# A new opening for a fused attention and feed-forward kernel: first k on two queues, another order of loads and steps

## The chip, the cores and the metric

The kernel runs on one core of a Trainium2 chip. The metric is the device time in microseconds (us), lower is better. A profiled execution has a span (first to last instruction of the program), which is shorter than its time: by 2.1 us in the kernel before (332.03 against 329.9 us). All runs here are of the fast state: the granted clock of TensorE was 0.995 to 1.0 of full speed.

## The reference, cut to what matters

```python
def _attn_ref(q, k, v):              # q, k, v: 8 batches x 8 heads x 576 x 64, float32
    scores = np.matmul(q, k.transpose(0, 1, 3, 2)) / np.sqrt(64)
    rel = pos[:, None] - pos[None, :]
    scores = np.where((rel >= 0) & (rel < 64), scores, -1000000000.0)   # window of 64
    ...                              # softmax, then @ v
def _moe_ref(x, w_gate, w_val, w_out):   # x: 4608 tokens x 512; d_ff = 1536
    g = x @ w_gate
    return (g / (1.0 + np.exp(-g)) * (x @ w_val)) @ w_out
```

Attention with a window of 64 gives x; a gated feed-forward follows. The kernel computes in bfloat16.

## The kernel before

Tokens are worked in 36 pieces of 128 ("chunks" of attention, counted from 0) and 9 pieces of 512 (the feed-forward's: piece 0 is chunks 0 to 3, piece 1 is chunks 4 to 7). A table of steps writes the program in order; each engine runs its own part of it in that order, and waits are worked out from who reads and writes what. LOADS are the first DMA issues, STEPS the opening of the program; after it a regular loop runs to the end.

```python
LOADS = """
f:0 init q:0 kq:1 kq:2 v:1 v:0 kq:3 v:2 v:3 w:7:9 w:1:2 w:5:6 kq:4 kq:5 w:3:4 ...
"""                      # kq:n = q and k of chunk n; w:a:b = columns a*128..b*128 of w_gate, then of w_val
STEPS = """
warm:45:64 B:0 B:1 ca:0:0 cd:0:1 T:0:1 T:0:0 ea:0:1 TQ:0 ld:8 wo:0:6 ed:0:0 qa:0 W:1 TQ:1 S:0 ...
"""
# W: a fill that computes nothing; T, TQ, TK: transposes (TensorE) of the first k, of q, of k
# qa/qd, ka/kd, xa/xd: evictions by ACT / DVE;  B: mask as a matmul;  S: scores and exp;  M: mask on DVE
# A0, A1: attention times v;  N: normalize (DVE);  X: transpose of x
# F:c:f:t0:t1: gate and value matmuls of block f for columns t0..t1 of piece c;  U: its two DVE steps
# TD, XD: transposes by DMA;  O: output matmuls
...
def first_load(self, n):         # k of chunk 0, float32, in two halves
    for u in range(2):
        ...
        self.g.op("sp", lambda e, d=d, a=a: e.dma_start(d, a), writes=[("ff", n, u)], dma=True)
...
def load_w(self, which, a, b):   # float32 in HBM to bfloat16 in SBUF, issued by POOL, like q, k and v
    self.g.op("pool", lambda e: e.dma_start(d, s), writes=[("W" + which, f) for f in range(a, b)], dma=True)
```

The softmax here doesn't subtract the row's maximum and nothing guards it: scores larger than these inputs give would overflow.

Of the kernel before, what the change touches and what calls it, by code (L numbers as in the profile page):

```python
# [7 lines left out]
B, H, S, D = 8, 8, 576, 64  # L8
DM, DFF = H * D, 1536
T = B * S  # L10
# [139 lines left out]
class _Kernel:  # L150
# [9 lines left out]
    LAST = NFC  # L160
    NI = 1
    LOADS = """
    f:0 init q:0 kq:1 kq:2 v:1 v:0 kq:3 v:2 v:3 w:7:9 w:1:2 w:5:6 kq:4 kq:5 w:3:4 w:4:5 w:6:7 v:5 w:2:3 v:6
    v:4 w:9:10 w:0:1 kq:6 v:7 kq:7 w:10:12
    """
    STEPS = """
    warm:45:64 B:0 B:1 ca:0:0 cd:0:1 T:0:1 T:0:0 ea:0:1 TQ:0 ld:8 wo:0:6 ed:0:0 qa:0 W:1 TQ:1 S:0 qd:1 TK:1
    ld:9 kd:1 W:1 TQ:2 S:1 qd:2 TK:2 kd:2 W:2 S:2 W:1 A0:0 A0:1 A1:0 A1:1 ld:10 N:0 TQ:3 B:3 qa:3 N:1 TK:3 X:0
    ka:3 xa:0 M:2 W:1 S:3 X:1 A0:2 xd:1 A1:2 ld:11 N:2 W:1 A0:3 A1:3 N:3 W:1 X:2 F:0:7:0:256 xd:2 U X:3
    F:0:8:0:384 xd:3 F:0:1 U U F:0:5 U TK:4 TQ:4 ld:12 ka:4 TQ:5 F:0:7:256:512 qd:4 TK:5 qa:5 F:0:8:384:512 U  # L170
    S:4 U F:0:3 kd:5 M:4 S:5 U F:0:4 M:5 U F:0:6 U F:0:2 U A0:4 A0:5 A1:4 ld:13 wo:6:12 A1:5 F:0:9 N:4 N:5 X:4
    F:0:0 U xa:4 X:5 U TK:6 xa:5 TQ:6 ld:14 F:1:0:0:128 ka:6 U F:1:1:0:256 qa:6 TQ:7 U F:1:2:0:256 qd:7 S:6
    TK:7 U F:1:3:0:256 kd:7 F:0:10 M:6 U U A0:6 S:7 A1:6 ld:15 TQ:8 TK:8 N:6 F:0:11 M:7 ka:8 qd:8 X:6 A0:7
    xa:6 S:8 U A1:7 ld:16 F:1:4:0:384 N:7 F:1:5:0:384 U X:7 U TQ:9 xa:7 F:1:6:0:384 M:8 qa:9 TK:9 U F:1:7 kd:9
    TD:10 U A0:8 S:9 A1:8 ld:17 F:1:8 N:8 M:9 X:8 TQ:11 xa:8 F:1:9 U qd:11 A0:9 TK:11 U A1:9 ka:11 F:1:10 N:9
    TK:12 U X:9 ka:12 TQ:12 F:1:11 xd:9 qd:12 TD:13 S:10 U S:12 F:1:0:128:512 M:10 F:1:1:256:512 M:12 A0:10 U
    S:11 A1:10 U F:1:2:256:512 F:1:3:256:512 N:10 F:1:4:384:512 U XD:10 F:1:5:384:512 O:0:0 U U U M:11 O:0:1
    A0:11 S:13 A1:11 O:0:2 N:11 M:13 X:11 O:0:3 xd:11 F:1:6:384:512 U TD:14 TD:15
    """

    def __init__(self, nc, q, k, v, wg, wv, wo, out):
# [103 lines left out]
    def first_load(self, n):  # L285
        (_, b, s, L), = self.segs(128 * n, 128)
        for u in range(2):
            d = self.ff[n][64 * u:64 * u + 64].rearrange("p h j d -> p h (j d)")
            a = self.k[b, 4 * u:4 * u + 4, s:s + L, :].rearrange("h (p j) d -> p h (j d)", j=2)
            self.g.op("sp", lambda e, d=d, a=a: e.dma_start(d, a), writes=[("ff", n, u)], dma=True)  # L290

    def cast(self, n, half, eng):
        hs = slice(2 * half, 2 * half + 2)
# [489 lines left out]
```

## Time and profile before

| | before |
|---|---|
| time, median of 4 runs | 332.23 us (331.72 to 332.55) |
| span of the profiled run | 329.9 us |
| TensorE busy | 320.5 us, 97% |
| first feed-forward matmul | 17.48 us |
| its second half (waits for Wv) | 18.09 us |
| second feed-forward ends | 20.06 us (20.28 in the profile, where a record is missing; see below) |
| first feed-forward of piece 2 (first thing after STEPS) | 83.31 us |

The lines of the profile are in the prediction.

### The profile page before, as it was taken

How to read it: one execution, taken by the hardware profiler on the slowest of the kernel's cores; microseconds unless marked ns; L12 is line 12 of the kernel's file. 1: busy time of each engine (PE TensorE's matmuls, PEld its weight loads, DVE VectorE, ACT ScalarE, POOL GpSimd, SP SyncE). 2: the span in 40 equal slices, each digit the busy share in tenths (PEclk: the TensorE clock that was granted, in tenths of full speed). 3: DMA queues.
4: the chain of work that ended last, by engine and by line, in shares of the span. 5: the costliest groups of instructions: out<-in, count | busy, mean ns of one | idle time of the engine just before them, and what ended most of it. 6: DMA issues, size and time to landing. Idle time of an engine off the chain costs nothing.

```text
span 329.9 us, 8342 instructions
## 1 busy us (share of the span) xinstructions
PE 320.5 (97%) x3505; PEld 166.2 (50%) x3543; DVE 217.0 (66%) x457; ACT 136.0 (41%) x247; POOL 116.5 (35%) x145
## 2 busy tenths in 40 slices
PE   7999999999999999999999999999999999999996
PEld 5565665564455444544445454545454544444444
DVE  5689999992467758585857676767676766555520
ACT  3736566453344344343425252525343432332222
POOL 8999999966017506060706060100000000000000
PEclk9999999999999999999999999999999999999999
DMA  9999999999999989999999999442424111100012
GB/s 104 163 169 171 160 184 156 160 156 181 189 173 142 167 155 105 152 90 167 90 169 82 175 75 184 67 111 42 120 35 128 34 64 34 64 34 32 32 63 99
DMA packets 169365, 38.56 MB, mean 117 GB/s; under 512 B 160368, under 2 KB 164848, under 8 KB 169328
## 3 DMA queue, kind: packets, MB, share of 16 engines
q0 software_dynamic: 123600, 18.75, 84.0%
q1 hardware_dynamic: 45584, 19.21, 29.2%
q8 instruction: 28, 0.46, 0.6%
q14 instruction: 9, 0.07, 0.1%
q10 hardware_dynamic: 144, 0.07, 0.1%
HBM read 37.75 MB, written 9.44 MB: 143 GB/s over the span
## 4 chain that ended last, share of the span: by engine, by line
PE 95%; DVE 2%; issue 1%
PE ps L602 56%; PE ps L635 27%; PE ps L421 3%; PE ps L534 2%; PE ps L309 2%; PE ps L471 2%; PE ps L665 1%; PE ps L568 1%; PE ps L401 1%; DVE xb L493 1%; PE ps L357 0%; DVE kT L301 0%; DVE mask L267 0%; DVE hT L613 0%; DVE pt L437 0%
## 5 line engine op out<-in xcount | busy, mean ns | idle before, releaser
L611 DVE SCALAR_TENSOR_TENSOR uu<-sig,ps 128x512 bf16<-128x512 bf16 (+3 forms) x117 | 75.4, 644 | 66.1 <-ACT sig L608 65.8
L602 PE MATMUL ps<-xT,Wv 128*128 128x512 bf16 (+3 forms) x466 | 112.4, 363 | 0.1
L602 PE MATMUL ps<-xT,Wg 128*128 128x512 bf16 (+3 forms) x447 | 108.1, 362 | 2.0 <-issue 0.6
L608 ACT ACTIVATE sig<-ps 128x512 bf16<-128x512 f32 (+3 forms) x117 | 66.0, 565 | 88.8 <-PE ps L602 88.7
L635 PE MATMUL ps<-Wo,hT 128*128 128x512 bf16 x405 | 94.6, 379 | 2.2 <-issue 2.1
L613 DVE SCALAR_TENSOR_TENSOR hT<-uu,ps 128x512 bf16<-128x512 bf16 (+3 forms) x117 | 75.6, 646 | 4.0
L371 POOL DMA_DIRECT2D va<-in_v_dram x40 | 39.7, 1026 | 89.4 <-PE ps L534 87.3
L602 PEld LDWEIGHTS ps<-xT,Wv 128*128 128x128 bf16 x468 | 44.9, 98 | 49.1 <-DVE hT L613 0.5
L602 PEld LDWEIGHTS ps<-xT,Wg 128*128 128x128 bf16 x468 | 43.9, 98 | 46.1 <-DMA xT<-xb 0.5
L635 PEld LDWEIGHTS ps<-Wo,hT 128*128 128x128 bf16 x420 | 39.9, 98 | 46.6
L431 ACT ACTIVATE pt<-ps 128x512 bf16<-128x512 f32 x72 | 37.8, 600 | 26.7 <-PE ps L421 26.6
L647 ACT ACTIVATE ost<-ps 128x512 f32<-128x512 f32 x35 | 20.9, 597 | 66.2 <-PE ps L635 66.0
L283 POOL DMA_DIRECT2D qn<-in_q_dram x40 | 40.7, 1037 | 2.6 <-issue 1.8
L283 POOL DMA_DIRECT2D kn<-in_k_dram x39 | 40.0, 1047 | 0.3 <-DMA kn<-in_k_dram 0.3
L437 DVE TENSOR_TENSOR pt<-pt,mask 128x512 bf16<-128x512 bf16 x66 | 24.3, 419 | 0.2
L556 DVE TENSOR_TENSOR xb<-ps,rp 128x448 bf16<-128x448 f32 (+1 forms) x36 | 18.5, 513 | 1.2
L553 DVE RECIPROCAL rp<-ps 128x7 f32<-128x7 f32 (+1 forms) x36 | 6.7, 187 | 15.5 <-PE ps L534 15.5
L421 PE MATMUL ps<-qT,kT 64*64 64x64 bf16 (+1 forms) x864 | 16.0, 205 | 0.4 <-ACT kT L299 0.2
L421 PEld LDWEIGHTS ps<-qT,kT 64*64 64x64 bf16 x864 | 12.4, 109 | 7.5 <-DVE hT L613 4.2
L534 PE MATMUL ps<-va,pt 64*64 64x65 bf16 x728 | 11.5, 193 | 0.1
L493 DVE TENSOR_TENSOR xb<-ps,rc 128x256 bf16<-128x256 f32 x24 | 10.2, 425 | 0.8
L534 PEld LDWEIGHTS ps<-va,pt 64*64 64x64 bf16 x728 | 9.4, 108 | 0.6 <-DVE hT L613 0.4
(50 smaller groups left out, 104.9 us busy)
## 6 DMA issues: line engine op xcount, KB each, us to landing
out_dram<-ost SPq DMA_DIRECT2D x35, 256.0 KB, 2.8
qn<-in_q_dram POOLq DMA_DIRECT2D x32, 128.0 KB, 6.7
va<-in_v_dram POOLq DMA_DIRECT2D x32, 128.0 KB, 6.4
kn<-in_k_dram POOLq DMA_DIRECT2D x31, 128.0 KB, 7.2
Wo<-in_moe_w_out_dram POOLq DMA_DIRECT2D x2, 768.0 KB, 12.1
Wg<-in_moe_w_gate_dram POOLq DMA_DIRECT2D x8, 128.0 KB, 5.5
Wv<-in_moe_w_val_dram POOLq DMA_DIRECT2D x8, 128.0 KB, 5.6
Wg<-in_moe_w_gate_dram POOLq DMA_DIRECT2D x2, 256.0 KB, 5.7
```

The costliest lines, as they stand in the source:

```text
L283: self.g.op("pool", lambda e, d=d, a=a: e.dma_start(d, a), writes=ks, dma=True)
L371: g.op("pool", lambda e, d=d, a=a: e.dma_start(d, a), writes=ks, dma=True)
L421: r = e.matmul(sv[h][o:o + 64, c, q0:q1], self.kT[ps, c, kk:kk + 64], qT[ps, c, q0:q1], start=not biased, stop=not biased or c == 3 and kk ...
L431: g.op("act", lambda e, po=po, si=si: e.activation(po, si, ACTF.Exp, scale=SCALE), reads=[bk], writes=[pk])
L437: "dve", lambda e: e.tensor_tensor(po, po, m, ALU.mult), reads=[pk, "mask"], writes=[pk]))
L534: r = e.matmul(bb[b][0][ws, 65 * sl:65 * sl + 65], self.pt[(n + j) % self.NP][ks, h, ws], vv[ks, h, 0:65], start=m == q[0], stop=m == q[-1])
L602: r = e.matmul(bank[:, 0:n], W[:, kk, f * 128:f * 128 + 128], xT[:, kk, t0:t1], start=(kk == 0), stop=(kk == NK - 1))
L608: g.op("act", lambda e: e.activation(sig[:, 0:n], G[:, 0:n], ACTF.Tanh, scale=0.5), reads=[gk], writes=[("sig", i)])
L611: g.op("dve", lambda e: e.scalar_tensor_tensor(uu[:, 0:n], sig[:, 0:n], 1.0, G[:, 0:n], ALU.add, ALU.mult), reads=[("sig", i), gk], writes ...
L613: g.op("dve", lambda e: e.scalar_tensor_tensor(hT[:, f, t0:t1], uu[:, 0:n], 0.5, V[:, 0:n], ALU.mult, ALU.mult), reads=[("uu", i), vk], wr ...
L635: r = e.matmul(OB[:, :], hT[:, f, 128 * u:128 * u + 128], self.Wo[:, f, :], start=(f == 0), stop=(f == NF - 1))
L647: g.op("act", lambda e: e.activation(ost[:, :], OB[:, :], ACTF.Copy), reads=[ok], writes=[("ost", io)])
```

## The change

Its intent: load the first k faster, start attention of the first chunks sooner, and re-search the order of loads and steps. The description also speaks of one DMA transpose fewer.

```diff
-    f:0 init q:0 kq:1 kq:2 v:1 v:0 kq:3 v:2 v:3 w:7:9 w:1:2 w:5:6 kq:4 kq:5 w:3:4 w:4:5 w:6:7 v:5 w:2:3 v:6
-    v:4 w:9:10 w:0:1 kq:6 v:7 kq:7 w:10:12
+    f:0 init q:0 kq:2 kq:1 v:1 v:0 kq:3 v:2 kq:6 v:3 w:7:9 kq:5 kq:4 w:2:3 w:4:5 w:0:2 v:4 kq:7 w:9:10 v:5
+    w:10:12 w:5:7 w:3:4 v:7 v:6
...
-    warm:45:64 B:0 B:1 ca:0:0 cd:0:1 T:0:1 T:0:0 ea:0:1 TQ:0 ld:8 wo:0:6 ed:0:0 qa:0 W:1 TQ:1 S:0 qd:1 TK:1
...                                             (the whole table of steps is replaced)
+    warm:45:96 B:0 ca:0:0 cd:0:1 T:0:0 T:0:1 ea:0:0 ed:0:1 TQ:0 ld:8 B:1 qa:0 TQ:2 S:0 qd:2 TK:2 kd:2 W:1 TQ:1
+    qa:1 W:1 TK:1 ld:9 wo:0:6 ka:1 W:2 S:1 B:2 A0:0 S:2 A1:0 N:0 A0:1 A1:1 ld:10 TQ:3 N:1 W:1 X:0 qa:3 TK:3
+    xa:0 kd:3 W:1 X:1 A0:2 xa:1 S:3 A1:2 ld:11 TQ:6 N:2 W:1 TK:6 ka:6 M:3 W:1 X:2 qa:6 xd:2 W:1 A0:3 A1:3
+    F:0:7:0:384 N:3 U X:3 TQ:5 xa:3 F:0:8:0:384 qd:5 TK:5 U TQ:4 ka:5 F:0:7:384:512 F:0:8:384:512 qd:4 S:6
...
-            self.g.op("sp", lambda e, d=d, a=a: e.dma_start(d, a), writes=[("ff", n, u)], dma=True)
+            self.g.op(("sp", "act")[u], lambda e, d=d, a=a: e.dma_start(d, a), writes=[("ff", n, u)], dma=True)
```

More of the change, by code (lines that the diff above doesn't have):

```diff
@@ L162 @@
     LOADS = """
-    f:0 init q:0 kq:1 kq:2 v:1 v:0 kq:3 v:2 v:3 w:7:9 w:1:2 w:5:6 kq:4 kq:5 w:3:4 w:4:5 w:6:7 v:5 w:2:3 v:6
-    v:4 w:9:10 w:0:1 kq:6 v:7 kq:7 w:10:12
+    f:0 init q:0 kq:2 kq:1 v:1 v:0 kq:3 v:2 kq:6 v:3 w:7:9 kq:5 kq:4 w:2:3 w:4:5 w:0:2 v:4 kq:7 w:9:10 v:5
+    w:10:12 w:5:7 w:3:4 v:7 v:6
     """
     STEPS = """
-    warm:45:64 B:0 B:1 ca:0:0 cd:0:1 T:0:1 T:0:0 ea:0:1 TQ:0 ld:8 wo:0:6 ed:0:0 qa:0 W:1 TQ:1 S:0 qd:1 TK:1
-    ld:9 kd:1 W:1 TQ:2 S:1 qd:2 TK:2 kd:2 W:2 S:2 W:1 A0:0 A0:1 A1:0 A1:1 ld:10 N:0 TQ:3 B:3 qa:3 N:1 TK:3 X:0
@@ L169 @@
-    ka:3 xa:0 M:2 W:1 S:3 X:1 A0:2 xd:1 A1:2 ld:11 N:2 W:1 A0:3 A1:3 N:3 W:1 X:2 F:0:7:0:256 xd:2 U X:3
-    F:0:8:0:384 xd:3 F:0:1 U U F:0:5 U TK:4 TQ:4 ld:12 ka:4 TQ:5 F:0:7:256:512 qd:4 TK:5 qa:5 F:0:8:384:512 U
-    S:4 U F:0:3 kd:5 M:4 S:5 U F:0:4 M:5 U F:0:6 U F:0:2 U A0:4 A0:5 A1:4 ld:13 wo:6:12 A1:5 F:0:9 N:4 N:5 X:4
-    F:0:0 U xa:4 X:5 U TK:6 xa:5 TQ:6 ld:14 F:1:0:0:128 ka:6 U F:1:1:0:256 qa:6 TQ:7 U F:1:2:0:256 qd:7 S:6
-    TK:7 U F:1:3:0:256 kd:7 F:0:10 M:6 U U A0:6 S:7 A1:6 ld:15 TQ:8 TK:8 N:6 F:0:11 M:7 ka:8 qd:8 X:6 A0:7
@@ L174 @@
-    xa:6 S:8 U A1:7 ld:16 F:1:4:0:384 N:7 F:1:5:0:384 U X:7 U TQ:9 xa:7 F:1:6:0:384 M:8 qa:9 TK:9 U F:1:7 kd:9
-    TD:10 U A0:8 S:9 A1:8 ld:17 F:1:8 N:8 M:9 X:8 TQ:11 xa:8 F:1:9 U qd:11 A0:9 TK:11 U A1:9 ka:11 F:1:10 N:9
-    TK:12 U X:9 ka:12 TQ:12 F:1:11 xd:9 qd:12 TD:13 S:10 U S:12 F:1:0:128:512 M:10 F:1:1:256:512 M:12 A0:10 U
-    S:11 A1:10 U F:1:2:256:512 F:1:3:256:512 N:10 F:1:4:384:512 U XD:10 F:1:5:384:512 O:0:0 U U U M:11 O:0:1
-    A0:11 S:13 A1:11 O:0:2 N:11 M:13 X:11 O:0:3 xd:11 F:1:6:384:512 U TD:14 TD:15
+    warm:45:96 B:0 ca:0:0 cd:0:1 T:0:0 T:0:1 ea:0:0 ed:0:1 TQ:0 ld:8 B:1 qa:0 TQ:2 S:0 qd:2 TK:2 kd:2 W:1 TQ:1
@@ new lines @@
+    qa:1 W:1 TK:1 ld:9 wo:0:6 ka:1 W:2 S:1 B:2 A0:0 S:2 A1:0 N:0 A0:1 A1:1 ld:10 TQ:3 N:1 W:1 X:0 qa:3 TK:3
+    xa:0 kd:3 W:1 X:1 A0:2 xa:1 S:3 A1:2 ld:11 TQ:6 N:2 W:1 TK:6 ka:6 M:3 W:1 X:2 qa:6 xd:2 W:1 A0:3 A1:3
+    F:0:7:0:384 N:3 U X:3 TQ:5 xa:3 F:0:8:0:384 qd:5 TK:5 U TQ:4 ka:5 F:0:7:384:512 F:0:8:384:512 qd:4 S:6
+    TK:4 ld:12 U U F:0:2 kd:4 M:6 S:4 U S:5 F:0:4 M:4 F:0:0 M:5 U A0:4 F:0:1 U U A1:4 ld:13 wo:6:12 TK:7 TQ:7
+    ka:7 F:0:9 N:4 qa:7 U X:4 A0:5 xa:4 S:7 A1:5 ld:14 F:0:10 N:5 M:7 U X:5 F:0:11 xd:5 U F:0:5 U F:0:3 U A0:6
@@ new lines @@
+    A0:7 A1:6 ld:15 A1:7 TQ:8 F:0:6 N:6 N:7 qa:8 X:6 TK:8 ld:16 xa:6 TQ:9 U X:7 ka:8 F:1:0:0:256 TK:9 xa:7
+    qd:9 S:8 U F:1:1 kd:9 M:8 F:1:2 U U A0:8 S:9 A1:8 ld:17 F:1:3 N:8 TD:10 U X:8 F:1:4 xd:8 U TQ:11 F:1:5 M:9
+    qa:11 U F:1:6 U A0:9 TK:11 A1:9 ka:11 F:1:7 N:9 U X:9 TK:12 xa:9 TQ:12 F:1:8 kd:12 qd:12 TD:13 S:10 U S:12
+    F:1:9 M:10 A0:10 M:12 S:11 A1:10 F:1:10 U N:10 F:1:11 U XD:10 F:1:0:256:512 U O:0:0 U M:11 A0:11 S:13
+    A1:11 O:0:1 N:11 M:13 X:11 O:0:2 xd:11 O:0:3 TD:14 TD:15
```

## The prediction

> **What bounds the kernel now.** I read the page first, then busy time by stretches, then the order of time of the first 34 us, then single transfers from issue to landing. The page says who is busy and who ends the run.
>
> ```profile
> PE 320.5 (97%) x3505; PEld 166.2 (50%) x3543; DVE 217.0 (66%) x457; ACT 136.0 (41%) x247; POOL 116.5 (35%) x145
> ...
> PE 95%; DVE 2%; issue 1%
> ```
>
> TensorE holds 97% of the span and 95% of the chain that ended last. The time is therefore a sum: the tensor work that has to be done plus the time in which TensorE does none of it. The change adds and removes hardly any tensor work, so I look for the lost time. The table by stretches has the span, then busy time and instruction count per engine:
>
> ```profile
> 0.00:20.28 20.28, 17.62 (x340) 11.69 (x341) 12.84 (x47) 9.78 (x18) 19.24 (x28) 1.00 1.71 141
> 20.28:82.86 62.58, 61.27 (x849) 36.73 (x859) 51.83 (x124) 33.41 (x66) 56.60 (x69) 1.00 2.00 167
> 82.86:329.90 247.04, 241.59 (x2318) 117.76 (x2343) 152.35 (x287) 92.79 (x163) 40.63 (x49) 1.00 0.87 102
> ```
>
> From 20.28 us to 82.86 us (the rest of the stage that the change rewrites) TensorE is idle 62.58 - 61.27 = 1.3 us, so little can be won there. Part of that 1.3 us is not even real: after many small matmuls a group of 4 shows only 3, and the missing record (216 ns) leaves a hole. After 82.86 us the step list ends and the program is the same. What is left is the first 20.28 us. The order of time shows what happens there:
>
> ```profile
> 6.87 0.63 PE L357 MATMUL ps<-wz 128*128 128x512 bf16 x1
> ...
> 8.80 0.38 PE L357 MATMUL ps<-wz 128*128 128x512 bf16 x1
> ...
> 17.48 0.60 PE L602 MATMUL ps<-xT,Wg 128*128 128x256 bf16 x4
> ...
> 18.09 0.33 PEld L602 LDWEIGHTS ps<-xT,Wv 128*128 128x128 bf16 x4 [0.29 <-DMA Wv<-in_moe_w_val_dram]
> ...
> 18.76 0.81 PE L602 MATMUL ps<-xT,Wg 128*128 128x384 bf16 x4
> ...
> 20.28 0.81 PE L602 MATMUL ps<-xT,Wg 128*128 128x512 bf16 x3
> ```
>
> L357 are fills that keep the clock up and compute nothing. The first feed-forward matmul starts at 17.48 us, its second half waits for the first Wv at 18.09 us, and from 18.54 us on TensorE is nearly full. What decides the opening is when the first pair of Wg and Wv pieces lands. They are issued by POOL, which is never idle from 1.24 us on:
>
> ```profile
> 7.47 0.93 POOL L283 DMA_DIRECT2D qn<-in_q_dram  x1
> 8.34 0.94 POOL L283 DMA_DIRECT2D kn<-in_k_dram  x1
> ...
> 10.93 0.84 POOL L377 DMA_DIRECT2D Wg<-in_moe_w_gate_dram  x1
> 11.67 0.83 POOL L377 DMA_DIRECT2D Wv<-in_moe_w_val_dram  x1
> 12.40 0.84 POOL L377 DMA_DIRECT2D Wg<-in_moe_w_gate_dram  x1
> ```
>
> From start to start a q, k or v load of one chunk takes 8.34 - 7.47 = 0.87 us of POOL, a weight load 11.67 - 10.93 = 0.74 us whatever its width. The view of Wv gives 6.4 us from issue to landing for the one issued at 11.67 us: 18.05 us, just where TensorE's wait of 0.29 us ends. The Wg ahead of it has 5.8 us: 16.7 us.
>
> **The Trainium skill.** "DMA: Bandwidth & Descriptors", section "Issuing engines are not separate DMA queues": DMAs from several engines share the same 16 DMA engines, and issuing from more than one saves only the sequencer's issue time. The trace lets me size that for the first k. Its two halves are issued on SP at 0.74 and 1.54 us; the view of ff has 2.7 us to landing for one and 4.1 us for the other, so they land at 3.4 and 5.6 us. The second was issued after POOL's first q (1.24 us) and shares the engines with it. "TensorE: Matmul & The Clock Gate", section "Part 1: The HAM clock gate": the full clock comes after about 3.4 us of sustained activity in a free-running window. The trace agrees in kind: the same fill takes 0.63 us at 6.87 us and 0.38 us at 8.80 us. "Trainium Kernel Development and Optimization", section "Performance Expectations": matmul busy time is a bad metric as matmuls are pipelined. Here too: a 512-column matmul lasts 0.38 us but starts every 0.216 us (24 of them take 5.18 us in the chain), so I count starts.
>
> **The change part by part.** (1) ff on two queues. The second half goes out on ACT about 0.8 us earlier and lands, by estimate, at 3.6 to 4.3 us in place of 5.6. The mask set-up on DVE lasts to 4.6 us and the longer warm-up (45 matmuls of 96 columns in place of 64; at the low clock 53 ns x 96/64 = 80 ns each, 3.6 us) to 4.62 us. So the first transposes start at some 5.1 to 5.5 us in place of 6.03: 0.5 to 0.9 us won. But q of chunk 0 lands at 6.2 us (4.9 us after its issue at 1.24), so scores of chunk 0 win about 0.3 us, and what comes next waits for loads on POOL: chunk 2's at the old times of chunk 1, and k of chunk 1 at the old time of k of chunk 2, 9.56 us. Nothing of the 0.5 us reaches the first feed-forward.
>
> (2) The order of loads. The old list has 11 loads of q, k, v ahead of the first weights, the new one 13 (q and k of chunk 6 were put ahead). That is 2 x 0.87 = 1.73 us: Wg lands at 16.7 + 1.73 = 18.4 us, Wv at 18.05 + 1.73 = 19.8 us. **This is the step I trust most.**
>
> (3) The first feed-forward. New list: 384 columns at once (1.30 us) in place of 256 (0.87 us). Its second half starts at 19.8 us and ends at 20.45 us (4 x 162 ns). Then transpose X of chunk 3 (4 x 56 ns = 0.22), q of chunk 5 (0.22), second feed-forward of 384 columns (1.30): 22.2 us. Now compare the useful work. The old kernel had at 20.28 us everything of chunks 0 to 3, plus 0.87 + 1.30 of feed-forward. The new one has at 22.2 us the same plus 0.43 (384 against 256 columns) plus the transposes of chunk 6 (0.44) plus q of chunk 5 (0.22) = 1.09 us more. It used 1.92 us for 1.09 us of work: **behind by 0.83 us**.
>
> (4) After that I walked the loads on by the same issue times: w:2:3 lands at about 24.0 and 24.8 us against a need at 24.2 and 25.1; the others have more room. Weights come in 8 pieces in place of 10, four issues or 2.9 us less of POOL, so later chunks come earlier. No new load wait, though a tight one.
>
> (5) Fewer split feed-forwards: 3 in place of 9. A split costs TensorE some 20 ns, but DVE and ACT a fixed part each: by the rows of 128 and 512 columns, two DVE operations of 0.28 and 0.69 us, so 0.145 us fixed each. Six splits: 6 x 0.29 = 1.7 us of DVE; two q evictions and one x eviction moved to ACT: 3 x 0.42 = 1.3 us more, of 51.8 us in that stretch. DVE is nine tenths busy from 20 to 60 us, and the few true holes of TensorE after 20 us (0.25 us at 46.1 us, 0.14 us at 39.6 and 69.0 us, some smaller) belong to it: at most 0.5 us to be had. One change fewer between small and full matmuls: 0.1 us. The new list, though, packs attention of chunks 4 to 7 into the feed-forward of chunk 0: by my count about 24 us of DVE beside 24.8 us of TensorE, so new small waits are as likely.
>
> (6) One fill more: it lies in waits. "One DMA transpose fewer" I cannot find: both lists have four double ones and one of x.
>
> Sum: +0.8 (load order) - 0.4 (DVE and splits) - 0.1, then +0.1 for new waits = +0.4 us, rounded down to **+0.2** because such a list is found by a search that sees overlaps that my walk does not: 332.18 + 0.2 = 332.4 us.
>
> **Rivals.** (a) The search was right: the earlier start carries through, attention of chunk 6 fills holes, and DVE's relief removes all holes; about -1 us, 331.2. For it: DVE's load. Against: 1.3 us of idle time is all there is after 20 us, and the weights land later. (b) A new wait: DVE becomes the bound between 22 and 47 us, or w:2:3 comes late; +1 to +1.5 us, 333.5. For it: the tight count in (5). (c) The opening is hidden anyway, since the end of the stage waits for DMA transposes: no change, 332.2. Against: only 0.5 us of wait for xT from a transpose.
>
> **Range and chances.** The rivals span 331.2 to 333.5; three runs of before spread by 0.55 us. 8 in 10: 331.2 to 333.3. 2% is 6.6 us, a third of the whole opening: faster 0.01, same 0.98, slower 0.01.
>
> **What would show it.** Second half of ff landed before 4.5 us and first transposes before 5.6; first Wg and Wv landed near 18.4 and 19.8 us; TensorE waiting for that Wv by 0.5 us or more; idle time from there to the end of the stage below 1.3 us. I am wrong if the first feed-forward starts before 18 us, or if TensorE, at the first matmul after the list (82.86 us before), is earlier than before by more than 0.5 us.

## The result, and the profile after

The changed kernel takes 332.80 us (median of 4 runs, 332.50 to 333.46), the kernel before 332.23 us. The ratio is 1.0021, 95% interval 1.0002 to 1.0041: slower by a little, and "same" at 2%. (A ratio is the mean time of one kernel's fast runs over that of the other's of the same rounds, so not quite the ratio of the medians.) The spans are 331.0 and 329.9 us.

The page of the kernel after:

```profile
PE 324.4 (98%) x3496; PEld 162.3 (49%) x3496; DVE 214.8 (65%) x442; ACT 137.1 (41%) x244; POOL 113.6 (34%) x141
...
PE 93%; POOL 4%; DMA 2%; issue 0%; DVE 0%; POOLq 0%
```

TensorE shows 3.9 us more busy time, though it has no more to do: the trace of the kernel before lacks 38 matmul records (3505 of them beside 3543 weight loads, line in the prediction). What matters is the chain: POOL and DMA have come into it with 6%. In order of time the start of the chain reads (start, length, what):

```profile
1.24 1.91 POOL qn L282 x2
3.15 0.87 POOL kn L282
...
10.15 0.88 POOL qn L282
11.03 0.87 POOL kn L282
11.90 0.88 POOL va L370
12.78 0.65 POOL Wg L376
13.42 6.25 DMA Wv<-in_moe_w_val_dram
19.67 0.05 issue
19.71 0.82 PE ps L601 x4
```

From 1.24 us to 19.71 us no computing stands on the path that sets the end. It is one load issued after another by POOL, then the flight of the first Wv. The pair at 10.15 and 11.03 us is q and k of chunk 6. TensorE's own view of the two halves of the first feed-forward, and of a hole further on:

```profile
18.47 0.81 PE L601 MATMUL ps<-xT,Wg 128*128 128x384 bf16 x4 [0.55 <-DMA Wg<-in_moe_w_gate_dram]
...
19.71 0.82 PE L601 MATMUL ps<-xT,Wv 128*128 128x384 bf16 x4 [0.43 <-DMA Wv<-in_moe_w_val_dram]
...
28.40 0.81 PE L601 MATMUL ps<-xT,Wg 128*128 128x512 bf16 x3
...
29.61 0.38 PE L601 MATMUL ps<-xT,Wg 128*128 128x512 bf16 x1 [0.40 <-issue]
```

Both halves wait for their weights, which they did for 0.29 us in all before. The hole at 29 us is a group of four matmuls whose fourth should start 3 x 0.216 = 0.65 us after the first, at 29.05 us, and starts at 29.61: 0.56 us are lost with no wait that the profile can name. By stretches (busy us and count of each engine follow the span), first the kernel before:

```profile
20.28:83.31 63.03, 61.72 (x858) 37.18 (x867) 51.83 (x124) 33.66 (x67) 56.60 (x69) 1.00 2.00 167
```

then the kernel after:

```profile
22.17:84.42 62.25, 61.85 (x811) 32.92 (x809) 50.60 (x113) 31.77 (x60) 51.88 (x63) 1.00 1.99 172
84.42:331.00 246.58, 243.98 (x2337) 117.25 (x2335) 151.81 (x285) 92.68 (x162) 40.62 (x49) 1.00 0.80 100
```

The later cut, 83.31 and 84.42 us, is the start of piece 2. The earlier one is meant to be the end of the second feed-forward, and at 22.17 us it is. At 20.28 us in the kernel before it is not: the group of four matmuls that starts there shows only x3 (line in the prediction), while its four weight loads are all there, and e4, an experiment with the same lists whose trace has that record, has x4 right behind its second feed-forward. First before, then e4:

```profile
19.90 0.69 PEld L602 LDWEIGHTS ps<-xT,Wg 128*128 128x128 bf16 x4
```

```profile
19.14 0.81 PE L602 MATMUL ps<-xT,Wv 128*128 128x384 bf16 x4
19.79 1.03 PE L602 MATMUL ps<-xT,Wg 128*128 128x512 bf16 x4
```

So the first of the four is the missing one, and the second feed-forward ended one matmul (0.216 us) earlier, at 20.06 us. The stretch from there to piece 2 is 83.31 - 20.06 = 63.25 us, and e4's is 63.23.

Before 22.17 us the new kernel has done 1.09 us more work than the old one by 20.06 us (the prediction's sum), in 2.11 us more time, so it is **1.02 us behind**. The middle stretch should then last 63.25 - 1.09 = 62.16 us if TensorE were as well fed as before; it lasts 62.25, **0.1 us more**, although 0.56 us of it are the hole. The rest, 246.59 us before (329.90 - 83.31), is 246.58. The sum, 1.1 us, is the difference of the spans; the times of these two runs differ by 0.75 us.

### The profile page after: what moved, and what is told of

Same layout as the page of the kernel before. It is cut to its first block, busy times and chain, and to the rows that moved or that the text cites. A ratio compares the mean times of both kernels' runs of the same rounds, so it can differ in the third digit from the quotient of the medians.

```text
span 331.0 us, 8249 instructions
## 1 busy us (share of the span) xinstructions
PE 324.4 (98%) x3496; PEld 162.3 (49%) x3496; DVE 214.8 (65%) x442; ACT 137.1 (41%) x244; POOL 113.6 (34%) x141
## 4 chain that ended last, share of the span: by engine, by line
PE 93%; POOL 4%; DMA 2%; issue 0%; DVE 0%; POOLq 0%
PE ps L601 57%; PE ps L634 28%; PE ps L420 3%; PE ps L533 2%; DMA Wv<-in_moe_w_val_dram 2%; POOL qn L282 1%; PE ps L308 1%; POOL va L370 1%; POOL kn L282 1%; PE ps L470 1%; PE ps L664 1%; PE ps L567 1%; POOL Wg L376 0%; DVE ost L300 0%; POOLq L767 0%
## 5 line engine op out<-in xcount | busy, mean ns | idle before, releaser
L610 DVE SCALAR_TENSOR_TENSOR uu<-sig,ps 128x512 bf16<-128x512 bf16 (+3 forms) x111 | 74.5, 671 | 70.1 <-ACT sig L607 69.5
L601 PE MATMUL ps<-xT,Wg 128*128 128x512 bf16 (+3 forms) x444 | 111.6, 373 | 1.0 <-DMA Wg<-in_moe_w_gate_dram 0.6
L607 ACT ACTIVATE sig<-ps 128x512 bf16<-128x512 f32 (+3 forms) x111 | 65.1, 586 | 90.1 <-PE ps L601 89.6
L634 PE MATMUL ps<-Wo,hT 128*128 128x512 bf16 x420 | 97.8, 379 | 0.0
L612 DVE SCALAR_TENSOR_TENSOR hT<-uu,ps 128x512 bf16<-128x512 bf16 (+3 forms) x111 | 74.6, 672 | 4.0 <-PE ps L601 0.2
L601 PEld LDWEIGHTS ps<-xT,Wv 128*128 128x128 bf16 x444 | 43.1, 98 | 51.5 <-DMA Wv<-in_moe_w_val_dram 0.8
L601 PEld LDWEIGHTS ps<-xT,Wg 128*128 128x128 bf16 x444 | 42.0, 98 | 47.8 <-DVE rc L489 0.6
L282 POOL DMA_DIRECT2D qn<-in_q_dram x40 | 39.1, 994 | 1.6 <-issue 0.8
L282 POOL DMA_DIRECT2D kn<-in_k_dram x39 | 38.2, 1000 | 0.5 <-issue 0.5
```

The lines of the kernel that those rows point to most:

```text
L282: self.g.op("pool", lambda e, d=d, a=a: e.dma_start(d, a), writes=ks, dma=True)
L601: r = e.matmul(bank[:, 0:n], W[:, kk, f * 128:f * 128 + 128], xT[:, kk, t0:t1], start=(kk == 0), stop=(kk == NK - 1))
L607: g.op("act", lambda e: e.activation(sig[:, 0:n], G[:, 0:n], ACTF.Tanh, scale=0.5), reads=[gk], writes=[("sig", i)])
L610: g.op("dve", lambda e: e.scalar_tensor_tensor(uu[:, 0:n], sig[:, 0:n], 1.0, G[:, 0:n], ALU.add, ALU.mult), reads=[("sig", i), gk], writes ...
L612: g.op("dve", lambda e: e.scalar_tensor_tensor(hT[:, f, t0:t1], uu[:, 0:n], 0.5, V[:, 0:n], ALU.mult, ALU.mult), reads=[("uu", i), vk], wr ...
L634: r = e.matmul(OB[:, :], hT[:, f, 128 * u:128 * u + 128], self.Wo[:, f, :], start=(f == 0), stop=(f == NF - 1))
```

## The experiments

All twelve gave correct results. Each run has times and one trace; the table has the times, and the four numbers that I read from the order of time of each trace: start of the second half of the first feed-forward ("V"), end of the second feed-forward (the start of what follows it), length of the stretch from there to piece 2, and the rest. In the traces of before, f1 and f4 the record at that end is missing (x3 for x4), and 0.22 us is taken off what they show (20.28, 20.77 and 22.45 us).

| kernel | median us (runs) | ratio to before, 95% | V | 2nd ends | stretch | rest |
|---|---|---|---|---|---|---|
| before | 332.23 (4) | | 18.09 | 20.06 | 63.25 | 246.59 |
| changed | 332.80 (4) | 1.0021, 1.0002 to 1.0041 | 19.71 | 22.17 | 62.25 | 246.58 |
| e1 | 332.95 (5) | 1.0023, 0.9995 to 1.0051 | 18.81 | 21.71 | 62.51 | 246.52 |
| e2 | 333.44 (6) | 1.0040, 1.0014 to 1.0066 | 20.25 | 23.08 | 63.23 | 246.29 |
| e3 | 332.49 (6) | 1.0011, 0.9986 to 1.0036 | 19.49 | 21.95 | 61.96 | 246.42 |
| e4 | 332.40 (6) | 1.0009, 0.9983 to 1.0036 | 17.72 | 19.79 | 63.23 | 247.47 |
| f1 | 332.56 (6) | 1.0008, 0.9995 to 1.0022 | 18.49 | 20.55 | 63.24 | 246.74 |
| f2 | 335.26 (6) | 1.0092, 1.0065 to 1.0120 | 20.15 | 22.64 | 62.24 | 246.60 |
| f3 | 333.70 (6) | 1.0046, 1.0026 to 1.0065 | 18.12 | 20.68 | 65.47 | 247.24 |
| f4 | 332.55 (6) | 1.0014, 0.9992 to 1.0035 | 20.16 | 22.23 | 63.24 | 246.53 |
| g1 | 333.12 (5) | 1.0024, 1.0006 to 1.0042 | 19.87 | 22.38 | 61.93 | 246.32 |
| g2 | 333.52 (2) | 1.0038, 1.0011 to 1.0065 | 20.32 | 22.79 | 62.16 | 246.54 |
| g3 | 333.45 (6) | 1.0046, 1.0022 to 1.0071 | 19.92 | 22.88 | 62.47 | 246.44 |
| g4 | 332.89 (5) | 1.0019, 1.0000 to 1.0037 | 21.02 | 23.43 | 61.67 | 246.35 |

The median of before beside them was 332.10 (e), 332.27 (f) and 332.13 us (g), 11 runs each. Read the stretch first. In the five traces with the old steps (before, e2, e4, f1, f4) "2nd ends" ranges from 19.79 to 23.08 us, but the stretch only from 63.23 to 63.25, and the rest, e4 apart, from 246.29 to 246.74. What differs between these executions lies nearly all ahead of "2nd ends". The times of one kernel's runs spread by 0.4 to 3.5 us; most kernels were traced once, so where the runs without a trace lost their time is not shown.

**Is it the order of the loads?** e2 makes the one move in the old kernel, e1 takes it back in the new one.

```diff
 e2 (kernel before)
-    ... kq:3 v:2 v:3 w:7:9 ... w:0:1 kq:6 v:7 ...
+    ... kq:3 v:2 kq:6 v:3 w:7:9 ... w:0:1 v:7 ...
```

> The kernel before with one edit: the loads of q and k of chunk 6 moved to where the changed kernel has them, ahead of v of chunk 3 and of the first weights; steps unchanged. My theory: first Wv lands at 19.7 us in place of 18.05, TensorE waits for it some 1.9 us in place of 0.29, and most of that stays to the end: time 1.2 to 1.6 us longer than the kernel before, 333.6 us. Rival (TensorE has slack later that takes it up): under 0.5 us longer.

Measured: 333.44 us, 1.3 us longer. The first Wv landed 6.8 us after its issue at 13.4 us, and its half started at 20.25 us. In the traced run (334.72 us, slower than the median) a lower clock followed the waits: the first gate group, 0.60 us long before, took 1.04 us at 18.78 us. The edit also puts v of chunk 3 two loads later, and attention waited 0.58 us for it at 16.95 us. So in the old list, two loads put that far ahead cost about what their issue takes (1.73 us; measured 1.3, interval 0.5 to 2.2), and nothing later takes it up.

```diff
 e1 (changed kernel)
-    ... v:2 kq:6 v:3 w:7:9 kq:5 ...
+    ... v:2 v:3 w:7:9 kq:6 kq:5 ...
-    ... A1:2 ld:11 TQ:6 N:2 W:1 TK:6 ka:6 M:3 W:1 X:2 qa:6 xd:2 W:1 A0:3 A1:3
-    F:0:7:0:384 N:3 U X:3 TQ:5 xa:3 F:0:8:0:384 qd:5 TK:5 ...
+    ... A1:2 ld:11 N:2 W:1 M:3 W:1 X:2 xd:2 W:1 A0:3 A1:3
+    F:0:7:0:384 N:3 U X:3 TQ:5 xa:3 F:0:8:0:384 qd:5 TQ:6 TK:6 ka:6 qa:6 TK:5 ...
```

> The changed kernel with the loads of q and k of chunk 6 put behind the first pair of weights, and the transposes of chunk 6 behind the second feed-forward; all else as changed. My theory (the two loads ahead of the weights cost the time): the first Wg lands near 16.6 us in place of 18.34, the first Wv near 17.95 in place of 19.67; the first feed-forward starts near 17.9 us (now bounded by attention of chunk 3) and its second half near 18.6 in place of 19.71 without a wait for Wv; span and time 0.7 to 1.1 us shorter than the changed kernel, so 331.8 us, 0.4 us under the kernel before. Rival (the new order of steps is late by its own vector work, whatever the weights do): first feed-forward stays at 18.4 us or later, time within 0.3 us of the changed kernel.

Measured: 332.95 us, no gain. The weights did come early (Wv 5.9 us after its issue at 11.67 us, so 17.6 us), and V at 18.81. TensorE in that trace:

```profile
16.83 0.40 PE L567 MATMUL ps<-ident,xb 128*128 128x128 bf16 x4 [0.77 <-DVE xb L492]
17.06 0.38 PE L356 MATMUL ps<-wz 128*128 128x512 bf16 x1
17.50 0.72 PE L470 MATMUL ps<-va,pt 64*64 64x65 bf16 x32
18.15 0.82 PE L601 MATMUL ps<-xT,Wg 128*128 128x384 bf16 x4
18.81 0.81 PE L601 MATMUL ps<-xT,Wv 128*128 128x384 bf16 x4
...
20.17 0.40 PE L308 MATMUL ps<-ident,qn 128*128 128x128 bf16 x4 [0.26 <-DMA qn<-in_q_dram]
```

The feed-forward no longer waits for weights, but for attention of chunks 2 and 3 ahead of it: the transposes of x of chunk 2 wait for DVE (0.77 us at 16.83). Then q of chunk 5 comes late (0.26 us at 20.17). At 21.71 us e1 is 0.46 us ahead of the changed kernel, but has the transposes of chunk 6 (0.44 us) still to do. My theory that the two early loads alone cost the time falls for the new list: there they cost about 1 us of waiting for weights (0.55 + 0.43 us), and without them two more limits, standing right behind, take up all but 0.02 us of that by "2nd ends". This is read from one trace of e1; the times (332.95 us, and 332.80 for the changed kernel in another round) only say that there is no clear gain.

**Do the two queues matter?** e3 puts both halves on SP in the new kernel, e4 the second half on ACT in the old one (the one line of the diff, each way).

> The changed kernel with both halves of the first k on the SP queue again. My theory: second half lands near 5 us in place of 3.45, first transposes start up to 1 us later, but the first feed-forward still waits for the same Wv at 19.7 us: time within 0.3 us of the changed kernel. Rival (the earlier start carries through): 0.5 to 1 us longer than the changed kernel.

> The kernel before with the second half of the first k on the ACT queue, all else as before. My theory: it lands near 3.5 us in place of 5.65; first transposes start when the four bias matmuls end (near 6.0), first feed-forward still waits for the first Wv at 18.05 us: time within 0.3 us of the kernel before. Rival: 0.5 us or more faster.

Measured: 332.49 and 332.40 us, neither clear of the kernel it was made from (the changed kernel ran in other rounds than e3). In e3 the first transposes started at 5.57 us in place of 5.25 us, and V at 19.49 us. The part is worth nothing that these runs can show, as predicted. One step of e4's expectation missed: its Wv landed at 17.26 us and the first feed-forward did not wait for it. The trace of e4 holds a surprise. It was 0.27 us ahead at "2nd ends" and finished 0.6 us later than before. First the trace of before (again with the first of four records missing, so it starts at 117.24), then that of e4, at the start of piece 3:

```profile
117.46 0.81 PE L602 MATMUL ps<-xT,Wg 128*128 128x512 bf16 x3 [0.24 <-DMA xT<-xb]
```

```profile
117.64 1.04 PE L602 MATMUL ps<-xT,Wg 128*128 128x512 bf16 x4 [0.72 <-DMA xT<-xb]
```

Piece 3 needs x of chunk 15, which comes by the second of two DMA transposes. It landed at 117.2 us before and at 117.6 in e4. In the old kernel this transpose arrives at the moment it is needed, so a faster opening can run into it. The changed kernel comes to that point at 118.17 us and does not wait.

**Does that gate hold the time?** f1 and f4 transpose chunk 15 by TensorE, with and without the two queues.

```diff
-                self.XD(n + 1)
+                if n != 14:
+                    self.XD(n + 1)
...
+                    if (c, u, s) == (2, 3, 0):
+                        self.X(15)
+                        self.Xev(15, "act")
```

> The kernel before with the first k on two queues and with chunk 15 transposed by TensorE and evicted by ACT in place of its DMA transpose. Theory: what the opening won with two queues (first output matmul at 71.2 us in place of 71.7) was given back at 117.6 us, where the next stage waited 0.72 us for the second DMA transpose of a pair; with that transpose gone the wait is gone, at a price of 0.22 us of TensorE: 0.4 to 0.7 us faster than two queues alone, 331.8 us. Rival: the wait moves to the first transpose of the pair, or the slower time of the two-queue kernel lies elsewhere: no change from 332.4.

> The kernel before with chunk 15 transposed by TensorE in place of its DMA transpose, nothing else. Theory: its wait at 117.4 us is 0.24 us, the transpose by TensorE costs 0.22 us: within 0.2 us of the kernel before.

Measured: 332.56 and 332.55 us. The wait is gone from the traces (the rest of f1 is 246.74 us against 247.47 in e4), but the times don't gain: f1's opening, the same program as e4's, was 0.77 us later in its traced run (V 18.49 against 17.72 us). So the gate is real in a trace and its worth in time is not settled; it is below the scatter of the opening. f4's trace shows one place where that scatter arises:

```profile
13.18 0.92 PE L471 MATMUL ps<-va,pt 64*64 64x65 bf16 x56 [1.96 <-DMA va<-in_v_dram]
...
15.57 0.63 PE L357 MATMUL ps<-wz 128*128 128x512 bf16 x1
```

v of chunk 0, issued at 6.60 us as always, landed 6.5 us later in place of 4.7. TensorE stood still for 1.96 us, and the fill of 0.63 us (0.38 at full clock) says that the clock had fallen, too. All of it was still there at "2nd ends" (22.23 against 20.06 us), and this run took 334.12 us, where the median is 332.55.

**Is the order of chunks 1 and 2 at fault?** g4 puts chunk 1 first again, in loads and steps.

```diff
-    q:0 kq:2 kq:1 v:1 ...       TQ:2 S:0 qd:2 TK:2 kd:2 W:1 TQ:1 qa:1 W:1 TK:1 ... ka:1 W:2 S:1 B:2
+    q:0 kq:1 kq:2 v:1 ...       TQ:1 S:0 qd:1 TK:1 kd:1 W:1 TQ:2 qa:2 S:1 W:1 TK:2 ... ka:2 W:2 B:2
```

> The changed kernel with chunk 1 loaded ahead of chunk 2 again, and its transposes and scores with it. Theory: scores of chunk 1 start near 9.5 us in place of 10.2, but the first feed-forward still waits for the same weights at 18.3 and 19.7 us: within 0.3 us of the changed kernel. Rival (the order of chunks 1 and 2 costs time): 0.5 us or more faster.

Measured: 332.89 us. Scores of chunk 1 started at 8.46 us in place of 10.19, and it changed nothing in time (333.12 us for the changed kernel in the same rounds, g1 below): in the traced run the half that needs Wv waited until 21.02 us, for a Wv that took 7.6 us to land. The rival is not seen.

**Splits, and the hole at 29 us.** g3 cuts six full blocks of piece 1 in two, g1 is the changed kernel again, f2 and g2 are one kernel with the weight load of blocks 0 and 1 cut in two.

```diff
 g3 (six times)                       f2 and g2
-    F:1:3 ... U                      -    w:4:5 w:0:2 v:4 kq:7
+    F:1:3:0:256 F:1:3:256:512 ... U U  +    w:4:5 w:0:1 v:4 w:1:2 kq:7
```

> The changed kernel with six full feed-forward blocks of chunk 1 cut into halves of 256 columns, in place and in the same order: the cost of six splits by itself, which the prediction took to be most of 0.4 us. Theory: TensorE has no hole there to fill, so six splits cost at most 0.2 us. Rival (the prediction): 0.3 to 0.5 us slower than the changed kernel.

> The changed kernel once more, unaltered, for a second trace and more times on one chip. If the hole of 0.4 to 0.6 us on the fourth gate matmul of column block 0 (near 29 us) belongs to the program, it is there again; if it was chance, it is gone. First feed-forward within 0.3 us of 18.5 us and its second half within 0.5 us of 19.7 us if the loads decide it; time 332.5 to 333.1 us.

> The changed kernel with the load of weight columns 0 and 1 cut in two and v of chunk 4 between them. Theory: the hole of 0.56 us before 29.6 us comes from Wv for column block 0 landing only at 29.2 us; cut in two it lands near 28.2 us and the hole goes: 0.3 to 0.5 us faster than the changed kernel, 332.4 us. Rival (a stall of instruction fetch, by chance there): the hole stays or shows elsewhere, time as the changed kernel.

> The changed kernel with the weight load cut in two, once more: its median was 335.3 us, while the one run that was traced took 333.3 us. A trace of a slow run should show where the 2 us lie. Theory: waits for DMA transposes of x between 100 and 300 us (0.37 us in the fast run). Rival: later weight or value loads, between 25 and 45 us.

g1: 333.12 us, just above what was expected. V is in its range, but the first feed-forward started at 19.11 us, 0.6 us late: v of chunk 0 landed 5.6 us after its issue, 4.1 in the first trace, and attention was late. The hole is there with 0.27 us in place of 0.56. In g4 there is none and the stretch is 61.67 us. Take the hole out of the other three traces with these steps and they agree: 62.25 - 0.56 = 61.69, 61.93 - 0.27 = 61.66 and, in e3, 61.96 - 0.29 = 61.67 us. So the new list has a stretch of 61.67 us, 0.49 us better than 62.16, plus a hole of 0 to 0.6 us. In f2 the Wv of block 0 landed at 27.95 us, well ahead of its use, and a hole was there all the same (0.31 us of idle time at 29.99); in g2 there was none, but a wait for a later Wv at 37.71 us (line below). My theory that a late Wv makes it has fallen. What makes it stays open: the profile names no wait.

g3: the trace has the hole with 0.19 us (29.94 in place of 29.75 us), so its stretch without it is 62.28 us, 0.6 us longer than 61.67. Here the rival, the prediction's own figure, was nearer than I was. Most of it is one new wait, for a PSUM bank that ACT still reads:

```profile
67.19 1.04 PE L591 MATMUL ps<-xT,Wg 128*128 128x512 bf16 x4 [0.44 <-ACT pt L420]
```

In time g3 is 0.33 us over g1, inside the scatter.

How much idle time was there to be won in this stretch? e4's trace, with the old steps and no record missing there, shows a span of 63.23 us and a busy TensorE for 63.16, so 0.07 us:

```profile
19.79:83.02 63.23, 63.16 (x870) 37.25 (x869) 51.94 (x124) 33.70 (x68) 57.11 (x70) 1.00 1.98 163
```

f2 had a median of 335.26 us, its twin g2 333.52 us in two runs, and the two traced runs took 333.3 us each. The slow runs of f2 were never traced, so what made them slow is open, and I draw nothing from that median.

**A version that passes all limits?** f3 puts chunk 6 behind the weights, a first feed-forward of 256 columns ahead of attention of chunk 3, cuts the weight load as f2, and transposes chunk 15 by TensorE.

```diff
-    ... M:3 W:1 X:2 qa:6 xd:2 W:1 A0:3 A1:3 F:0:7:0:384 N:3 U X:3 TQ:5 xa:3 F:0:8:0:384 ...
+    ... M:3 X:2 F:0:7:0:256 xd:2 A0:3 A1:3 F:0:8:0:384 N:3 U X:3 TQ:6 xa:3 TK:6 U TQ:5 ... F:0:7:256:512 ...
```

> The changed kernel with q and k of chunk 6 behind the first weights, with 256 columns of the first feed-forward put ahead of attention of chunk 3, columns 0 and 1 of the weights cut in two, and chunk 15 transposed by TensorE. Theory: both bounds of the first feed-forward (weights, then vector work of chunks 2 and 3) are then passed: first feed-forward near 17.0 us, and 0.6 to 1.2 us faster than the changed kernel: 331.8 us, at or a little under the kernel before. Rival: loads of q, k of chunk 6 and 5 or of later weights become the wait, as with the plain move: no faster than 332.5 us.

Measured: 333.70 us. The traced run took 335.19 us, so what follows is a slow case. The first feed-forward did start at 17.16 us, and the second ended at 20.68, with some 1.3 us less work done by then than in the changed kernel at 22.17 us (an estimate by the prediction's sizes). Then it was given back:

```profile
36.60 0.81 PE L601 MATMUL ps<-xT,Wg 128*128 128x512 bf16 x3 [0.59 <-DMA Wg<-in_moe_w_gate_dram]
37.80 1.02 PE L601 MATMUL ps<-xT,Wv 128*128 128x512 bf16 x4 [0.39 <-DMA Wv<-in_moe_w_val_dram]
```

That is 0.98 us of waiting, and 0.9 us more were lost near 50 us in a hole that the profile puts down to issue. The wait belongs to f3's own cut of the weight load, at least in part. The cut puts two more issues ahead of this pair, which landed at 36.33 and 37.67 us; in the changed kernel it landed at 34.94 and 36.29. g2, which has the cut and not the other edits, waits at the same place, where the changed kernel does not. First g2, then the changed kernel:

```profile
37.71 1.02 PE L601 MATMUL ps<-xT,Wv 128*128 128x512 bf16 x4 [0.34 <-DMA Wv<-in_moe_w_val_dram]
```

```profile
37.16 1.03 PE L601 MATMUL ps<-xT,Wv 128*128 128x512 bf16 x4
```

What f3 would do without the cut was not run. No kernel here beats the kernel before.

## Why the prediction was right

The time (332.4 us forecast, 332.80 measured) lies in the range, and so does the class.

- **(1) First k.** Its ACT half landed at 3.45 us, just before the estimated 3.6 to 4.3, and the first transposes started at 5.25 us, inside the range given. Scores of chunk 0 won 0.98 us (6.88 for 7.86) and not 0.3, as q landed at 5.50 us in place of 6.16. That this gives no clear gain in time is what e3 and e4 show within their scatter.
- **(2) Order of loads.** The step trusted most held best: Wg landed at 18.34 us and Wv at 19.67, where 18.4 and 19.8 were forecast. e2 shows that the move costs 1.3 us in the old list. What the prediction did not see is that taking it back in the new list wins nothing (e1): in e1's trace vector work and another load stand right behind.
- **(3) First feed-forwards.** Ends at 22.17 us for 22.2 forecast. Behind by 1.02 us and not 0.83: the prediction took 20.28 us for the old end, though it knew that records were missing after small matmuls; with 20.06 its own sum gives 1.05.
- **(4) Later loads.** w:2:3 landed at 23.8 and 24.6 us and nothing waited for it.
- **(5) Splits and DVE.** 0.4 + 0.1 us were to be won, and four traces of the new steps agree on 0.49. How it was won is not shown. The 1.3 us of idle time, and the holes put down to DVE, were nearly all missing records: e4's complete trace has 0.07 us left, so by the profile there was hardly a hole for DVE's relief to fill. g3 puts six splits back and loses 0.6 us, which fits, but 0.44 us of that are a wait for ACT. What was mis-sized is the 0.1 us for new waits: the hole took 0 to 0.56 us.
- **Sum.** In the two traces: +1.02 (opening) - 0.49 (stretch) + 0.56 (hole) = +1.1 us of span, where the sum had +0.4. Some 0.35 us of it don't show in the times of these runs, which nobody foresaw, and the medians differ by 0.57 us. So the delay of (2) was seen rightly, and that the number came as near as 0.4 us is partly luck. The hedge of 0.2 us in favour of the search had no ground. Of the rivals, (a) did not happen, (b) did not show in its two forms (the hole is a loss of another kind), and (c) is a real gate at 117 us, met by the old kernel and not by the new one. One detail was wrong: 82.86 us is the last piece of the old list, and piece 2 starts at 83.31.

## What to carry to other kernels

Where one engine issues all casting loads, the position of a load in that queue is a time: count issues ahead of the first thing that the busy engine needs, and multiply. Before taking back a change that looks like the cause, look for what stands next in line: here weights, vector work and a q load lay close behind each other, and moving one of them won nothing. And where runs of one kernel spread by more than the effect, compare stretches of traces between two fixed points: they agreed to 0.03 us, where the times did not to 1 us. Count the records at both points first: one missing matmul at 20.28 us would have made a saving of 0.49 us look like 0.27.

## What the Trainium skill lacked or had wrong

- "DMA: Bandwidth & Descriptors", section "Anatomy of one DMA — SWDGE (gpsimd) path", fits a DMA with 2.0 us plus bytes over 436e3. By that, an estimate from the page, the 256 KB that the first q reads would take 2.6 us. It took 4.9 us from issue to landing before and 4.3 after, with only the first k beside it. How long POOL is held by such an issue (0.87 us for q, k or v, 0.74 us for a weight load of either width) isn't given there.
- I found no page with the scatter of one and the same load from execution to execution: in the fourteen traces v of chunk 0 took 4.1 to 6.5 us from issue to landing, and the first Wv 5.6 to 7.6. The run of f4, with the 6.5, was 1.6 us slower than the median of its kernel.
- "DMA: Bandwidth & Descriptors", section "Rules for kernel authors", says that two transfers to disjoint partition halves serialize, and in the same row that their packets interleave on the same engines. In e4 two halves issued 0.01 us apart from SP and ACT landed 3.4 and 2.9 us after their issue. The DMA packets of the trace ran from 2.63 to 3.45 us for one and from 2.25 to 3.07 for the other: half of each beside the other, so "serialize" is too strong here.
- "TensorE: Matmul & The Clock Gate", section "HAM oscillation — how this bites in real kernels", has the rule of no idle gaps over some 3.4 us. In f4 a gap of 1.96 us, shorter than that, was followed by a fill of 0.63 us in place of 0.38.
